# Turning batch 1's keys and queries by the DMA crossbar in two parts, loading the later batches later, and broadcasting g by a transfer

## The chip, the cores and the metric

The kernel runs on one core of a Trainium2 chip. The metric is the device time of one execution in microseconds (us), as the median of several runs. The kernel before takes 218.26 us (216.22 to 218.64, 3 runs).

A run's *state* is called slow when it lies more than 1.5% above the fastest run of the same kernel. Medians and ranges below are over all runs; ratios use fast runs alone. All other times are from one profiled execution of each kernel, counted from the start of its span.

Some words that come back: a *hole* is a stretch in which TensorE idles; a transfer *lands* when its data has arrived; to *turn* is to transpose; the *granted clock* is the recorded share of TensorE's full clock, and *half clock* a stretch in which that share is 0.50.

## The reference

Four batches of eight heads, 768 tokens, head dimension 64. Each chunk of 32 queries attends to 8 memory keys, its own chunk, 16 tokens to the left and 8 to the right. The result passes through a normalised MLP with a residual:

```python
for c in range(768 // 32):
    l_start, r_end = max(0, 32*c - 16), min(768, 32*c + 32 + 8)
    k_full = concat([mem_k, k[:, :, l_start:r_end]]); v_full = concat([mem_v, v[:, :, l_start:r_end]])
    scores = q[:, :, 32*c : 32*c+32] @ k_full.T / sqrt(64)
    out[:, :, 32*c : 32*c+32] = softmax(scores) @ v_full
x  = heads side by side            # (4, 768, 512)
xn = (x - mean) / sqrt(var + 1e-6) * g
return x + relu(xn @ w_ch1) @ w_ch2   # 512 -> 2048 -> 512
```

## The kernel before

The 24 tiles of 128 tokens are worked in eight units of three. Unit `u` runs the MLP of its own tiles; the attention of the next unit's tiles is threaded between its matmuls. The position is a *step*: steps 0 to 15 are the first matmul (`up`), 16 to 27 the second (`down`). `at(step, fn, ...)` puts a piece of other work behind that step in program order:

```python
def attend(steps, kind="dma"):
    for i, (s0, s1, s2, s3) in enumerate(steps):
        t = following[i]
        at(s0, scores, ...); at(s1, values, ...); at(s2, norm, ...)
        at(s3, turn_x, u + 1, i, t % 6, kind)     # xn -> xT, for the next unit's up
        at(min(s3 + 3, 27), root, ...)
```

The program's order is also the order in which GpSimd and SyncE issue their transfers: in the changed kernel the transposes at 102.76 us stand behind the store at 102.25 us on SyncE. A batch's keys and queries reach the layout that the scores need (`KT`, `QT`: head dimension on the partitions) in one of two ways. Batches 0 and 1 are turned by TensorE. Batches 2 and 3 come token by token and are turned by the crossbar of the DMA:

```python
def load_tokens(b, which, t):       # GpSimd's queue: 128 tokens x 8 heads
    nc.gpsimd.dma_start(out=free(dst, 512 * t, ...), in_=dram(src, ...))
def cross_k(b, half, t0, t1):       # SyncE's queue
    nc.sync.dma_start_transpose(out=free(KT[b % 2], ...), in_=kraw[b % 2][...])
def k_around(b, t0, t1): ...        # GpSimd: four copies of the neighbours' edges inside KT
def load_v_head(b, h):              # GpSimd's queue: one head's own rows of V
    nc.gpsimd.dma_start(out=V[b % 2][16:80, :, h, 0:64], in_=dram(v, ...))
def v_around(b):                    # SyncE's queue: the neighbours' rows, SBUF to SBUF
    nc.sync.dma_start(out=vt[0:16, 1:NG, :, :], in_=vt[64:80, 0 : NG - 1, :, :])
    nc.sync.dma_start(out=vt[80:88, 0 : NG - 1, :, :], in_=vt[16:24, 1:NG, :, :])
```

So batch 2 needs a chain: token loads, crossbar transposes, edge copies, value loads (behind these copies on GpSimd), neighbour copies, values. The old plan spread it over three units:

```python
elif u == 1: ...
    for t in range(6):
        for which in range(2): at(14, load_tokens, 2, which, t)
if u == 2:
    cross((0, 0, 1, 1), 2, 0, 4, 3)
    at(8, k_around, 2, 0, 4)
    for h in range(H): at(8, load_v_head, 2, h)
    cross((14, 14, 15, 15), 2, 4, 6, 6)
elif u == 3:
    at(1, v_mem, 2); at(1, v_around, 2)
    at(4, k_around, 2, 4, 6)
    # attend: scores of the first tile at step 9, its values at step 14
```

At the start TensorE runs ten filler matmuls (`stay_busy(10)`) until the memory keys and K have landed.

The softmax here doesn't subtract the row's maximum and nothing guards it: scores larger than these inputs give would overflow.

## Time and profile before

| | before |
|---|---|
| median of 3 runs | 218.26 us |
| span of the profiled run | 214.4 us |
| first up matmul of unit 0 | 19.91 us |
| lengths of units 0 to 7 | 27.22, 26.98, 23.41, 23.13, 23.27, 23.13, 23.13, 24.26 us |

A unit runs from its first `up` matmul to the next unit's. First the clock in 40 slices, then the engines' totals in units 3 and 4 (stretch, its length, busy time and instructions of PE, its weight loads, DVE, ACT and POOL, then the granted TensorE clock, the DMA share, which is summed packet time over 16 engines' time and can exceed 1, and GB/s):

```profile
PEclk9999999999999999999999999999999999999999
...
97.52:120.65 23.13, 23.13 (x209) 13.40 (x208) 11.87 (x26) 9.73 (x20) 5.19 (x10) 1.00 0.41 75
120.65:143.92 23.27, 23.27 (x210) 13.37 (x209) 11.67 (x27) 9.17 (x20) 16.91 (x27) 1.00 2.00 164
```

TensorE is busy for the whole of both (23.13 of 23.13). Batch 2's chain: SyncE's transposes, GpSimd's edge copies and value loads, and TensorE's values (start, duration, what, how often, and in brackets the idle time just before and what ended it):

```profile
75.77 2.74 SPq L253 DMA_TRANSPOSE KT<-kraw  x2
```

```profile
80.75 0.79 POOL L274 COPY KT<-KT 128x192 f16<-128x192 f16 x3 [1.03 <-DMA KT<-kraw]
81.48 5.98 POOL L122 DMA_DIRECT2D V<-in_v_dram  x8
```

```profile
108.06 0.70 PE L307 MATMUL att<-V,AT 104*64 104x65 f16 x32
...
120.65 2.11 PE L375 MATMUL mm<-xT,w1c 128*128 128x384 f16 x12
```

The value loads start at 81.48 and the values at 108.06. Neither the values nor the first up matmuls of unit 4 (the last line) wait for anything.

### The profile page before, as it was taken

Reading aid. Unit: us, or ns where it says so; the run is one execution under the profiler, and the core shown is the slowest. Engines: PE = TensorE matmul, PEld = TensorE weight load, DVE = VectorE, ACT = ScalarE, POOL = GpSimd, SP = SyncE. Lnnn points to the kernel's source line nnn. Section 1 sums busy time; section 2 is a strip of 40 time slices with the busy share of each in tenths; the row PEclk is TensorE's granted clock in tenths of the full one; section 3 lists DMA queues with packets and bytes.
Section 4 is the critical chain, followed back from the end, with each engine's and each line's share of the span. In section 5 each row is a group of like instructions: output and inputs, shape, how many; then the busy total and the mean of one; then the engine's idle time right before and its main releaser. Section 6 shows DMA issues by size and latency. Waiting matters only on the chain.

```text
span 214.4 us, 5336 instructions
## 1 busy us (share of the span) xinstructions
PE 208.1 (97%) x2173; PEld 123.6 (58%) x2173; DVE 113.2 (53%) x268; ACT 91.1 (42%) x187; POOL 91.5 (43%) x169
## 2 busy tenths in 40 slices
PE   7889999999999999999999999999999999999993
PEld 2446775457755566546654566447644665457553
DVE  3748583685747548524375349324474447534222
ACT  4255445855573677202653167103661265303200
POOL 7992244689999319810004999520121000400000
PEclk9999999999999999999999999999999999999999
DMA  5999999999999959995313999997694101330012
GB/s 79 162 128 202 206 214 185 191 206 238 145 141 172 138 163 125 115 205 139 54 26 78 144 182 153 155 170 92 168 146 132 54 3 24 85 115 0 0 52 98
DMA packets 87611, 27.26 MB, mean 127 GB/s; under 512 B 78289, under 2 KB 84081, under 8 KB 87538
## 3 DMA queue, kind: packets, MB, share of 16 engines
q0 software_dynamic: 62128, 14.38, 75.3%
q1 hardware_dynamic: 25458, 12.54, 26.4%
q8 instruction: 17, 0.28, 0.5%
q14 instruction: 8, 0.07, 0.1%
HBM read 28.84 MB, written 6.29 MB: 164 GB/s over the span
## 4 chain that ended last, share of the span: by engine, by line
PE 91%; DMA 3%; DVE 2%; POOL 1%; issue 1%; ACT 1%; POOLq 0%; DVEq 0%; ACTq 0%
PE mm L375 38%; PE mm L392 38%; PE att L307 4%; PE att L287 3%; DMA kraw<-in_k_dram 3%; PE att L187 2%; PE mm L410 2%; PE mm L364 2%; PE mm L187 1%; DVE xn L327 1%; DVE xs L318 1%; PE att L350 1%; ACT AT L294 1%; PE mm L533 0%; PE att L364 0%
## 5 line engine op out<-in xcount | busy, mean ns | idle before, releaser
L375 PE MATMUL mm<-xT,w1c 128*128 128x384 f16 (+2 forms) x528 | 87.9, 322 | 0.1
L392 PE MATMUL mm<-w2c,rT 128*128 128x512 f16 x368 | 84.2, 379 | 0.0
L375 PEld LDWEIGHTS <-w1c 128*128 128x128 f16 x528 | 57.9, 114 | 24.7 <-issue 0.6
L381 ACT ACTIVATE rT<-mm 128x384 f16<-128x384 f32 (+2 forms) x66 | 31.7, 484 | 75.2 <-PE mm L375 53.8
L392 PEld LDWEIGHTS <-rT 128*128 128x128 f16 x368 | 34.5, 98 | 38.4
L383 DVE TENSOR_SCALAR rT<-mm 128x384 f16<-128x384 f32 (+2 forms) x66 | 35.6, 542 | 33.6 <-PE mm L375 33.3
L399 DVE SCALAR_TENSOR_TENSOR osb<-mm,rstd,xs 128x512 f32<-128x512 f32 x23 | 17.3, 751 | 42.4 <-PE mm L392 31.1
L294 ACT ACTIVATE AT<-att,band 104x512 f16<-104x512 f32 x48 | 29.5, 688 | 10.9 <-PE att L287 9.2
L336 POOL TENSOR_SCALAR veps<-squares 128x1 f32<-128x1 f32 x24 | 5.2, 216 | 52.1 <-ACT junk L333 50.8
L116 POOL DMA_DIRECT2D V<-in_v_dram x24 | 19.0, 796 | 12.1 <-DMA w1c<-in_moe_w_ch_dram 8.2
L333 ACT ACTIVATE junk<-xs,nmean 128x512 f16<-128x512 f32 x24 | 17.4, 724 | 7.7 <-DVE nmean L324 6.9
L327 DVE SCALAR_TENSOR_TENSOR xn<-xs,nmean,g_row 128x512 f16<-128x512 f32 x24 | 18.0, 752 | 0.9
L318 DVE SCALAR_TENSOR_TENSOR xs<-att,rec 128x512 f32<-128x512 f32 x24 | 16.6, 691 | 0.8
L274 POOL COPY KT<-KT 128x128 f16<-128x128 f16 (+4 forms) x16 | 4.3, 294 | 23.8 <-DMA KT<-kraw 23.8
L340 POOL TENSOR_TENSOR rstd<-veps,mhalf 128x1 f32<-128x1 f32 x24 | 13.2, 551 | 2.0
L122 POOL DMA_DIRECT2D V<-in_v_dram x16 | 12.0, 804 | 0.5 <-issue 0.4
L307 PEld LDWEIGHTS <-AT 104*64 104x64 f16 x384 | 7.5, 111 | 7.2 <-issue 3.0
L247 POOL DMA_DIRECT2D qraw<-in_q_dram x12 | 11.3, 943 | 0.0
L247 POOL DMA_DIRECT2D kraw<-in_k_dram x12 | 11.3, 940 | 0.0
L307 PE MATMUL att<-V,AT 104*64 104x65 f16 x384 | 9.5, 197 | 0.6 <-ACT AT L294 0.6
L364 PE MATMUL mm<-busy 128*128 128x512 f16 x26 | 8.8, 472 | 1.2 <-DVE counts L456 1.2
L287 PEld LDWEIGHTS <-KT 64*128 64x128 f16 x384 | 6.5, 95 | 5.9 <-issue 5.8
(76 smaller groups left out, 115.0 us busy)
## 6 DMA issues: line engine op xcount, KB each, us to landing
out_dram<-osb SPq DMA_DIRECT2D x23, 256.0 KB, 2.8
V<-in_v_dram POOLq DMA_DIRECT2D x36, 96.0 KB, 6.1
w1c<-in_moe_w_ch_dram POOLq DMA_DIRECT2D x4, 512.0 KB, 10.0
w2c<-in_moe_w_ch_dram POOLq DMA_DIRECT2D x4, 512.0 KB, 15.0
kraw<-in_k_dram POOLq DMA_DIRECT2D x12, 128.0 KB, 5.4
qraw<-in_q_dram POOLq DMA_DIRECT2D x12, 128.0 KB, 5.5
qraw<-in_q_dram POOLq DMA_DIRECT2D x3, 384.0 KB, 13.5
kraw<-in_k_dram POOLq DMA_DIRECT2D x3, 256.0 KB, 5.7
```

The costliest lines, as they stand in the source:

```text
L116: nc.gpsimd.dma_start(out=V[b % 2][r : r + hi - lo, g, :, 0:64], in_=dram(v, b * H * HS + lo * D, [[64, hi - lo], [HS, H], [1, 64]]),)
L247: nc.gpsimd.dma_start(out=free(dst, 512 * t, [[64, H], [1, 64]]), in_=dram(src, b * H * HS + 128 * t * D, [[D, 128], [HS, H], [1, 64]]),)
L294: nc.scalar.activation(out=free(a, 32 * c, [[512, 2], [64, 8], [1, 32]], KR), in_=free(p, 32 * c, [[512, 2], [64, 8], [1, 32]], KR), func= ...
L307: nc.tensor.matmul(out=p[64 * gg : 64 * gg + 64, h // 4, c0 : c0 + 65], lhsT=AT[t % 3][0:KR, h % 2, 4 * gg + h // 2, :], rhs=V[b % 2][0:KR ...
L318: nc.vector.scalar_tensor_tensor(out=x.rearrange("p (h d) -> p h d", h=H), in0=free(p, 0, [[128, H], [1, 64]]), scalar=1.0, in1=free(r, 0, ...
L327: nc.vector.scalar_tensor_tensor(out=xn[i], in0=x, scalar=nmean[i], in1=g_row, op0=ALU.add, op1=ALU.mult,)
L333: nc.scalar.activation(out=junk, in_=xs[xi], func=ACTF.Square, bias=nmean[i], accum_out=squares[i],)
L375: nc.tensor.matmul(out=p, lhsT=free(w, i, [[4, 128]]), rhs=xT[u % 2][:, dt, lo:hi], start=(dt == 0), stop=(dt == 3),)
L381: nc.scalar.activation(out=o, in_=p, func=ACTF.Relu)
L383: nc.vector.tensor_scalar(out=o, in0=p, scalar1=0.0, scalar2=None, op0=ALU.max)
L392: nc.tensor.matmul(out=p, lhsT=rT[hc][:, 128 * i : 128 * i + 128], rhs=w2c[hc // 4][:, hc % 4, :], start=(hc == 0), stop=(hc == 15),)
L399: nc.vector.scalar_tensor_tensor(out=o, in0=p, scalar=rstd[t % 9], in1=xs[t % 9], op0=ALU.mult, op1=ALU.add,)
```

## The change

Its intent: take batch 1's 128 TensorE transposes off the busiest engine by using the crossbar for batch 1 as well (in two parts, tiles 0 to 3 and 4 to 5). Batch 1's tokens then need the queues at the time at which batch 2's were loaded, so batch 2's chain moves later, and the attention steps of units 1 to 3 move with it. Unit 0's and 1's square sums and roots are placed by hand. At the start, g reaches all partitions by a transfer instead of an fp32 matmul. The core of the diff:

```diff
-    nc.vector.memset(ones32, 1.0)
+    nc.sync.dma_start(out=g_row, in_=dram(moe_g_ln, 0, [[0, 128], [1, 512]]))
     nc.sync.dma_start(out=memk32, ...)
-    nc.sync.dma_start(out=g_one, in_=dram(moe_g_ln, 0, [[0, 1], [1, 512]]))
...
-    nc.tensor.matmul(out=banks[2], lhsT=ones32, rhs=g_one, start=True, stop=True)
-    vec(out=g_row, in_=banks[2])
...     # u == 0
-            for h in (0, 4):
-                for which in range(2):
-                    at(15, load_kq, 1, which, 0, 96, h, h + 4)
+            for t in range(6):
+                for which in range(2):
+                    at(15, load_tokens, 1, which, t)
...     # u == 1
-            for j in (0, 2):
-                at(5 + 3 * j, kq_block, 1, j, 0, NG, "att")
-            for t in range(6):
-                for which in range(2):
-                    at(14, load_tokens, 2, which, t)
-            attend(((16, 19, 19, 22), (16, 19, 20, 23), (21, 23, 23, 26)), "att")
+            cross((1, 1, 2, 2), 1, 0, 4, 3)
+            at(3, k_around, 1, 0, 4)
+            for g in range(6):
+                at(3, load_v_group, 1, g)
+            cross((24, 24, 25, 25), 1, 4, 6, 6)
+            attend(((18, 22, 22, 24), (18, 22, 23, 25), (23, 25, 25, 27)), "att")
...     # u == 2
+            attend(((4, 9, 9, 9), (4, 9, 10, 10), (11, 15, 15, 15)))       # was 2, 7, 7, 7 ...
-                cross((0, 0, 1, 1), 2, 0, 4, 3)
-                at(8, k_around, 2, 0, 4)
-                    at(8, load_v_head, 2, h)
-                cross((14, 14, 15, 15), 2, 4, 6, 6)
+                for g in range(6, NG):
+                    at(0, load_v_group, 1, g)
+                        at(0, load_tokens, 2, which, t)
+                cross((23, 23, 24, 24), 2, 0, 4, 3)
...     # u == 3
+            attend(((11, 18, 18, 18), (11, 18, 19, 19), (20, 24, 24, 24)))  # was 9, 14, 14, 14 ...
-                at(1, v_around, 2)
+                at(0, k_around, 2, 0, 4)
+                    at(0, load_v_head, 2, h)
+                at(11, v_around, 2)
+                cross((14, 15, 16, 17), 2, 4, 6, 6)
```

More of the change, by code (lines that the diff above doesn't have):

```diff
@@ L49 @@
     g_row = sb.tile([128, 512], FP32, name="g_row")
-    g_one = sb.tile([1, 512], FP32, name="g_one")
-    ones32 = sb.tile([1, 128], FP32, name="ones32")
     busy = sb.tile([128, 512], FP16, name="busy")
@@ L242, in place @@
     def place(b, g):
-        return g if b < 2 else g % 2 * (NG // 2) + g // 2
+        return g if b < 1 else g % 2 * (NG // 2) + g // 2
     def load_tokens(b, which, t):
@@ L331, in root, with squared @@
     def root(t, xi):
+        squared(t, xi)
+        rooted(t, xi, nc.gpsimd)
+    def squared(t, xi):
         i = t % 3
@@ L335, in root, with rooted @@
         )
-        nc.gpsimd.tensor_scalar(
+    def rooted(t, xi, eng):
+        i = t % 3
+        eng.tensor_scalar(
             out=veps[i], in0=squares[i], scalar1=1.0 / 512, scalar2=1e-6,
@@ L339, in root @@
         )
-        nc.gpsimd.tensor_tensor(out=rstd[xi], in0=veps[i], in1=mhalf, op=ALU.pow)
+        eng.tensor_tensor(out=rstd[xi], in0=veps[i], in1=mhalf, op=ALU.pow)
     def turn_x(u, i, t, kind="att"):
@@ L524 @@
         turn_kq(first_k[j], k16[0], j, CUT[0])
-    stay_busy(4, spare)
+    stay_busy(3, spare)
     for j in range(2, 4):
@@ L532 @@
         keep_q(on[j], first_q[j], 0, j, CUT[1], 0, 6)
-    nc.tensor.matmul(out=banks[2], lhsT=ones32, rhs=g_one, start=True, stop=True)
-    vec(out=g_row, in_=banks[2])
+    stay_busy(3, spare)
     scores(0, 0)
@@ L580, in attend @@
                 at(s3, turn_x, u + 1, i, t % 6, kind)
-                at(min(s3 + 3, 27), root, t % 6, t % 9)
+                if u:
+                    at(min(s3 + 3, 27), root, t % 6, t % 9)
         def cross(steps, b, t0, t1, t2):
@@ L593 @@
             at(14, nc.vector.memset, memv16[:, :, :, 64:HD], 1.0)
-            at(23, clear_v, 1, nc.gpsimd)
+            at(12, clear_v, 1, nc.gpsimd)
             for j in (0, 2):
@@ L598 @@
             for t in range(3):
-                at(19 + t, root, t, t)
-            for h in (0, 4):
-                for which in range(2):
-                    at(15, load_kq, 1, which, 0, 96, h, h + 4)
-            for g in range(6):
-                at(23, load_v_group, 1, g)
-            attend(((17, 19, 19, 22), (17, 21, 21, 24), (20, 23, 23, 26)), "att")
-            at(26, mem_cols, 1)
-            at(26, v_mem, 1)
-        elif u == 1:
-            for j in (0, 2):
-                at(5 + 3 * j, kq_block, 1, j, 0, NG, "att")
-                at(7 + 3 * j, keep_rest)
-            for g in range(6, NG):
-                at(0, load_v_group, 1, g)
+                at(12 + t, squared, t, t)
+                at(14, rooted, t, t, nc.gpsimd)
             for t in range(6):
                 for which in range(2):
-                    at(14, load_tokens, 2, which, t)
-            attend(((16, 19, 19, 22), (16, 19, 20, 23), (21, 23, 23, 26)), "att")
-        elif following:
-            if u in (2, 4):
+                    at(15, load_tokens, 1, which, t)
+            attend(((17, 19, 19, 22), (17, 21, 21, 24), (20, 23, 23, 26)), "att")
+            at(16, mem_cols, 1)
+            at(20, v_mem, 1)
+        elif u == 1:
+            for t in range(3, 6):
+                at(t - 3, squared, t, t)
+                at(2, rooted, t, t, nc.gpsimd)
+            cross((1, 1, 2, 2), 1, 0, 4, 3)
[4 more added lines that the diff above has]
+            attend(((18, 22, 22, 24), (18, 22, 23, 25), (23, 25, 25, 27)), "att")
+        elif following:
+            if u == 2:
+                attend(((4, 9, 9, 9), (4, 9, 10, 10), (11, 15, 15, 15)))
+            elif u == 3:
+                attend(((11, 18, 18, 18), (11, 18, 19, 19), (20, 24, 24, 24)))
+            elif u == 4:
                 attend(((2, 7, 7, 7), (2, 7, 8, 8), (9, 13, 13, 13)))
@@ L623 @@
             if u == 2:
-                cross((0, 0, 1, 1), 2, 0, 4, 3)
-                at(8, mem_cols, 2)
-                at(8, k_around, 2, 0, 4)
-                for h in range(H):
-                    at(8, load_v_head, 2, h)
-                cross((14, 14, 15, 15), 2, 4, 6, 6)
-            elif u == 3:
-                at(1, v_mem, 2)
-                at(1, v_around, 2)
-                at(4, k_around, 2, 4, 6)
+                at(0, k_around, 1, 4, 6)
+                for g in range(6, NG):
[4 more added lines that the diff above has]
+                cross((23, 23, 24, 24), 2, 0, 4, 3)
+                at(20, mem_cols, 2)
+            elif u == 3:
+                at(0, k_around, 2, 0, 4)
+                for h in range(H):
+                    at(0, load_v_head, 2, h)
+                at(11, v_mem, 2)
+                at(11, v_around, 2)
+                cross((14, 15, 16, 17), 2, 4, 6, 6)
+                at(23, k_around, 2, 4, 6)
                 for t in range(6):
```

## The prediction

> **What bounds the kernel now.** I read the page's busy line first, then the chain that ended last, then what TensorE waited for, then the engines' timelines in the stretch that the change touches. The kernel works in eight units of three 128-token tiles. A unit has 28 steps, steps 0 to 15 the first matmul ("up") and 16 to 27 the second ("down"), and the attention of the next unit is threaded between them. The busy line and the chain's shares by engine:
>
> ```profile
> PE 208.1 (97%) x2173; PEld 123.6 (58%) x2173; DVE 113.2 (53%) x268; ACT 91.1 (42%) x187; POOL 91.5 (43%) x169
> ...
> PE 91%; DMA 3%; DVE 2%; POOL 1%; issue 1%; ACT 1%; POOLq 0%; DVEq 0%; ACTq 0%
> ```
>
> TensorE is busy 97% and is 91% of the chain. From the pieces of the chain (start, duration, what):
>
> ```profile
> 11.67 1.05 PE mm L533 x2
> ...
> 51.19 1.48 PE att L187 x64
> ...
> 56.69 1.48 PE att L187 x64
> ...
> 87.32 10.36 PE mm L392 x48
> ```
>
> The third and second lines are batch 1's 128 TensorE transposes, 2.96 us on the chain. L533 is the fp32 matmul that broadcasts g. The last line gives a down step: 4 of 48 matmuls, 10.36/12 = 0.863 us. An up step is 3.90/6 = 0.65 us (six of them before 51.19). What the matmuls themselves waited for, in all:
>
> ```profile
> PE mm L364 <- DVE counts L456: 1.2, 1, 1.2
> PE mm L187 <- DMA kraw<-in_k_dram: 1.1, 2, 0.6
> PE att L307 <- ACT AT L294: 0.6, 1, 0.6
> ```
>
> All three lie before 15 us. From there the old schedule hides every wait, so whatever the new one exposes is a loss in full. How narrowly it hides them is seen in unit 1, VectorE first, then TensorE (start, duration):
>
> ```profile
> 66.03 0.69 DVE L318 SCALAR_TENSOR_TENSOR xs<-att,rec 128x512 f32<-128x512 f32 x1
> ...
> 67.85 0.69 DVE L318 SCALAR_TENSOR_TENSOR xs<-att,rec 128x512 f32<-128x512 f32 x1
> ...
> 69.98 0.75 DVE L399 SCALAR_TENSOR_TENSOR osb<-mm,rstd,xs 128x512 f32<-128x512 f32 x1 [0.46 <-PE mm L392]
> ```
>
> ```profile
> 68.64 0.39 PE L350 MATMUL att<-identity,xn 128*128 128x128 f16 x4
> ```
>
> There are two attention buffers in PSUM. The transpose at 68.64 takes the one that VectorE finished reading at 67.85+0.69 = 68.54: 0.1 us of slack.
>
> **What the Trainium skill says.** "TensorE: Matmul & The Clock Gate", Back-to-back issue gap, gives an isolated gap of about 216 ns for 512 columns; 863/4 = 216 ns here agrees (its sustained 131 ns isn't seen). "DMA: Bandwidth & Descriptors", DMA Transpose (X-bar), says that the plain DMA transpose can be issued only from the sync and scalar engines; here all 31 stand on SyncE's in-order queue, behind the stores. The same page, Anatomy of one DMA, puts a fixed 2 us or so on a transfer, mostly for its completion; here a value load in a quiet queue lands 2.9 us after its issue began, and a crossbar transpose about 3.5 us. The same page, Issuing engines are not separate DMA queues, says all queues share 16 engines; here token loads that land 0.84 us apart land about 1 us further apart for each output store beside them.
>
> **The change part by part.**
> *Start.* The g matmul (1.05 us) goes, and net two filler matmuls of about 0.21 us come; at most 0.55 us is gained, since the scores then wait for the Q copy that ends at 12.27. The second matmul of unit 0 starts its third part at 40.85, and its weights landed at 40.61, so about 0.2 us survives. The g transfer runs while the DMA engines are less than half busy. Sum -0.2.
>
> *Unit 1, gain.* The transposes go: -2.96.
>
> *Unit 1, tokens.* GpSimd reaches its first batch 1 load at about 37.2 + 2.4 (clearing V) + 2.8 (three roots) = 42.4 us. Twelve token loads at 0.87 each; the seventh, which the K transpose needs, is issued at 47.6. Queued behind w2 and memory values (until 44.4), with three stores beside it, it lands at about 46.5 + 6x0.84 + 3x0.94 = 54.3. SyncE then issues four transposes at 1.27-1.3 each; the last Q one starts at 58.5 and lands at 62. Scores are due at 47.1 + 16x0.65 + 0.2 + 3x0.863 = 60.3. So a wait of 0.3 to 2.2: I take +1.3. The V loads, behind the K edge copies on GpSimd, start near 61 and just make step 22.
>
> *Unit 1, norms.* Values now come at step 22 and the turning at 24, where it was 19 and 22. VectorE has two norms (1.9 us each) in that time, and now the output combine of step 23 (0.75) stands between them in program order. The second buffer comes free 0.1 + 1.9 + 0.75 + 0.93 = 3.7 us after the values, and TensorE wants it after two down steps, scores and slack, 2.25: +1.4. The third tile's values are at step 25 and its turning at 27: the norm needs 2.07 (70.48 to 72.55 before) against 1.73, +0.35; and the xT copy (ends 1.0 us after the turning starts, 73.02 to 74.02) has no step behind it any more, +0.75. Together +2.5.
>
> *Unit 2.* V groups 6 to 11 are issued at its start, behind the third root and the edge copies (GpSimd free about 76.5). The fourth is issued 2.3 later and lands 2.9 after that, 81.7; its values are due near 81.2: +0.5.
>
> *Unit 3, the largest.* Batch 2's K transposes move from step 0 to step 23 of unit 2, behind a store: they start 3.45 - 1.3 = 2.15 us before unit 3 starts. Before, the value loads began 5.7 us after K's transposes (75.77 to 81.48, the edge copies between), so they begin at +3.55; eight at 0.75, the last at +8.8, landed at +11.7. Only then can the neighbouring values be copied. SyncE before:
>
> ```profile
> 99.98 0.60 SPq L130 DMA_DIRECT2D V<-V  x1
> 100.63 1.68 SPq L131 DMA_DIRECT2D V<-V  x1
> ```
>
> The DMA between 104 and 107 us, in 40 slices of 0.075 us:
>
> ```profile
> DMA  0000000000000499809000000000000000000000
> ```
>
> Its last packets end at about 105.5, 5.5 us after the first issue. I take 4.6 for the new order, in which the memory rows no longer stand ahead: ready at +16.5. The values are due at step 18, 16x0.65 + 0.57 + 3x0.863 = +13.6: a wait of +3.0. In the old schedule they came 2 us after the packets. The third tile's values then come at step 24, and its turning by DMA landed 4.43 us after the values before (114.67 to 119.10); three steps are left, 2.6: +1.85.
>
> Sum: -0.2 - 2.96 + 1.3 + 2.5 + 0.5 + 3.0 + 1.85 = +6.0. From unit 4 on nothing is added: batch 3's loads shift about as far as TensorE does.
>
> **The rivals.** *Clean gain:* every new wait is hidden and only the removed work counts: 218.3 - 3.2 = 215.1. For it: TensorE is the bound everywhere, and the steps look chosen to fit arrivals (7 steps between the neighbour copies and the values). Against it: those steps count from step 11 of unit 3, while the loads before it can't have landed by then. *Gain given back:* unit 1's waits eat the transposes, and the batch 2 waits are small because the neighbour copies take some 3 us when nothing stands ahead of them and the loads land early: 218 to 219.5. For it: the gap of 1.5 us in the queue before the last copy's packets is unexplained. *A pile-up:* 256-byte token loads, V loads and stores in 42 to 62 us delay the scores by 3 us more, and all else follows: 225 to 227. For it: the DMA digits are at 9 until 75 us. Against: batch 1's old loads occupied the queue for about the same 10 us.
>
> **Range and chances.** Most terms are estimates from neighbouring rows, and waits in series partly cover each other (a late unit 1 gives unit 2's loads time), so I take 5 of the 6 us: 218.3 + 5 is 223.3, and since the single profiled run of before was at the low side, 216.1, I say 223.0. Low 218.5 (second rival), high 226.5 (third). 2% is 4.4 us, just under my centre: slower 0.60, within 0.37, faster 0.03.
>
> **What would show it.** The transposes of batch 1 gone from the chain, 2.96 us. TensorE's busy share down to about 95%. In unit 1, idle time before the scores, ended by the Q transpose or edge copies, and before the first turning, ended by VectorE. In unit 3, a hole of about 3 us before the values, ended by the neighbour copy, and one of nearly 2 at the start of unit 4, ended by the xT transpose. If TensorE has no hole near its 110th microsecond, the largest term is wrong, and the kernel is about even; if it has none in unit 1 either, it is 3 us faster.

## The result, and the profile after

The changed kernel takes 239.01 us (237.23 to 239.80, 3 runs): 9.6% longer, ratio 1.0956 (95% interval 1.0843 to 1.1069). A ratio here is the mean time of one kernel's fast runs over that of the other's fast runs of the same rounds, so not quite the ratio of the medians. The span of the profiled run went from 214.4 to 238.1 us, 23.7 us more.

The page of the changed kernel, the lines that answer to those of before (busy time by engine; TensorE's busy share and its granted clock in 40 slices of 6 us; the chain by engine):

```profile
PE 215.6 (91%) x2045; PEld 124.7 (52%) x2045; DVE 107.6 (45%) x254; ACT 88.3 (37%) x183; POOL 101.1 (42%) x185
...
PE   6899999999879899999808939999999999999994
...
PEclk9659999999997999999985986999999999999999
...
PE 55%; DMA 26%; POOL 12%; issue 3%; DVE 1%; SPq 1%; ACT 1%; POOLq 0%; ACTq 0%; DVEq 0%
```

TensorE has 128 instructions fewer (2173 to 2045), yet is busy 7.5 us *longer* (208.1 to 215.6). The third line says why: in slices 2, 3, 13, 21, 22, 24 and 25 the clock is below 9 tenths. Before, all 40 digits were 9. In the trace the low stretches are 7.4 to 17.6, 72.2 to 75.7, 123.4 to 130.3 and 140.5 to 147.3 us, at *half clock* (a *granted clock*, the recorded share of TensorE's full clock, of 0.50). What the matmuls waited for (us in total, times, longest; the fillers' wait at the very start and four under 1 us left out):

```profile
PE att L305 <- DMA V<-V: 7.6, 1, 7.6
PE mm L380 <- DMA xT<-xn: 4.1, 1, 4.1
PE att L305 <- DMA V<-in_v_dram: 2.3, 3, 1.2
...
PE mm L185 <- DMA kraw<-in_k_dram: 1.2, 1, 1.2
...
PE att L285 <- DMA QT<-qraw: 0.7, 2, 0.4
...
```

The two long holes, and units 3 and 4 as a whole (columns as for these units of the kernel before):

```profile
115.66 2.75 PE L397 MATMUL mm<-w2c,rT 128*128 128x512 f16 x12
125.98 1.09 PE L305 MATMUL att<-V,AT 104*64 104x65 f16 x32 [7.57 <-DMA V<-V]
127.00 3.50 PE L397 MATMUL mm<-w2c,rT 128*128 128x512 f16 x8
...
141.54 4.00 PE L380 MATMUL mm<-xT,w1c 128*128 128x384 f16 x12 [4.07 <-DMA xT<-xn]
```

```profile
104.56:141.54 36.98, 25.34 (x210) 14.05 (x208) 12.70 (x27) 9.72 (x20) 15.46 (x27) 0.89 1.15 126
141.54:167.39 25.85, 25.85 (x208) 14.20 (x209) 11.01 (x26) 9.27 (x20) 14.64 (x26) 0.89 1.61 141
```

Read the durations, not only the brackets: eight `down` matmuls take 3.50 us behind the first hole, where eight take 1.90 us at full clock. Unit 4 has no idle time (25.85 busy of 25.85), and is 2.58 us longer than before with the same number of matmuls.

The chain into the first hole, SyncE's queue and GpSimd's:

```profile
102.76 3.25 SPq L251 DMA_TRANSPOSE KT<-kraw  x2
...
120.02 0.60 SPq L128 DMA_DIRECT2D V<-V  x1
```

```profile
107.22 0.40 POOL L272 COPY KT<-KT 128x256 f16<-128x256 f16 x1 [6.33 <-DMA KT<-kraw]
108.23 0.79 POOL L272 COPY KT<-KT 128x192 f16<-128x192 f16 x3 [0.62 <-DMA KT<-kraw]
108.97 5.97 POOL L120 DMA_DIRECT2D V<-in_v_dram  x8
```

The value loads begin at 108.97, directly behind the edge copies, which waited 6.33 us for the transposes. The last load lands at 119.81, the neighbour copy goes out at 120.02 and lands at 125.79, the values start at 125.98. Each link follows the one before at once. From the value loads to the values there are now 17.0 us; before there were 26.6, with slack.

Where the 23.7 us lie, by the starts of the units:

| | before | after | difference |
|---|---|---|---|
| first up | 19.91 | 23.65 | +3.74 |
| unit 0 | 27.22 | 27.21 | 0.0 |
| unit 1 | 26.98 | 29.86 | +2.88 |
| unit 2 | 23.41 | 23.85 | +0.44 |
| unit 3 | 23.13 | 36.98 | +13.85 |
| unit 4 | 23.27 | 25.86 | +2.59 |
| units 5 to 7 | 70.52 | 70.70 | +0.2 |

### The profile page after: what moved, and what is told of

Its sections match the earlier page's. It is cut to its first block, busy times and chain, and to the rows that moved or that the text cites. A ratio compares the mean times of both kernels' runs of the same rounds, so it can differ in the third digit from the quotient of the medians.

```text
span 238.1 us, 5078 instructions
## 1 busy us (share of the span) xinstructions
PE 215.6 (91%) x2045; PEld 124.7 (52%) x2045; DVE 107.6 (45%) x254; ACT 88.3 (37%) x183; POOL 101.1 (42%) x185
## 4 chain that ended last, share of the span: by engine, by line
PE 55%; DMA 26%; POOL 12%; issue 3%; DVE 1%; SPq 1%; ACT 1%; POOLq 0%; ACTq 0%; DVEq 0%
PE mm L397 25%; PE mm L380 23%; DMA V<-in_v_dram 13%; POOL V L114 4%; DMA KT<-kraw 3%; DMA w1c<-in_moe_w_ch_dram 3%; DMA kraw<-in_k_dram 3%; PE att L305 3%; DMA V<-V 2%; DMA xT<-xn 2%; PE att L285 2%; PE mm L415 1%; POOL kraw L245 1%; POOL qraw L245 1%; POOL V L120 1%
## 5 line engine op out<-in xcount | busy, mean ns | idle before, releaser
L380 PE MATMUL mm<-xT,w1c 128*128 128x384 f16 (+2 forms) x528 | 89.4, 327 | 4.8 <-DMA xT<-xn 4.1
L397 PE MATMUL mm<-w2c,rT 128*128 128x512 f16 x368 | 87.2, 389 | 0.0
L380 PEld LDWEIGHTS <-w1c 128*128 128x128 f16 x528 | 58.5, 115 | 31.2 <-issue 7.8
L305 PE MATMUL att<-V,AT 104*64 104x65 f16 x384 | 10.5, 201 | 10.1 <-DMA V<-V 7.6
L272 POOL COPY KT<-KT 128x128 f16<-128x128 f16 (+4 forms) x24 | 6.3, 294 | 28.8 <-DMA KT<-kraw 28.8
L305 PEld LDWEIGHTS <-AT 104*64 104x64 f16 x384 | 8.2, 114 | 17.3 <-issue 14.2
L245 POOL DMA_DIRECT2D kraw<-in_k_dram x18 | 16.9, 936 | 0.3 <-DMA kraw<-in_k_dram 0.3
L245 POOL DMA_DIRECT2D qraw<-in_q_dram x18 | 16.8, 936 | 0.0
L315 DVE RECIPROCAL rec<-att 128x8 f32<-128x8 f32 x24 | 4.9, 203 | 25.9 <-PE att L305 22.2
L345 POOL TENSOR_TENSOR rstd<-veps,mhalf 128x1 f32<-128x1 f32 x24 | 13.8, 575 | 2.0
L285 PEld LDWEIGHTS <-KT 64*128 64x128 f16 x384 | 7.6, 101 | 7.8 <-issue 7.0
```

The source lines that it names most:

```text
L245: nc.gpsimd.dma_start(out=free(dst, 512 * t, [[64, H], [1, 64]]), in_=dram(src, b * H * HS + 128 * t * D, [[D, 128], [HS, H], [1, 64]]),)
L305: nc.tensor.matmul(out=p[64 * gg : 64 * gg + 64, h // 4, c0 : c0 + 65], lhsT=AT[t % 3][0:KR, h % 2, 4 * gg + h // 2, :], rhs=V[b % 2][0:KR ...
L380: nc.tensor.matmul(out=p, lhsT=free(w, i, [[4, 128]]), rhs=xT[u % 2][:, dt, lo:hi], start=(dt == 0), stop=(dt == 3),)
L397: nc.tensor.matmul(out=p, lhsT=rT[hc][:, 128 * i : 128 * i + 128], rhs=w2c[hc // 4][:, hc % 4, :], start=(hc == 0), stop=(hc == 15),)
```

## The experiments

There were fifteen runs in five groups. Each group has its own runs of the kernel before on the same chip (medians 217.57, 217.72, 217.82, 216.87 and 217.06 us). All results were correct. The theory at the outset: the lateness of batch 2's chain makes the two holes, the holes make the clock drop, and something about g makes the late start. The rivals: batch 1's own transfers do the harm, or the late start is chance.

### Batch 2's lateness alone, in the kernel before

```diff
# u == 1
-            for t in range(6):
-                for which in range(2):
-                    at(14, load_tokens, 2, which, t)
# u == 2, u == 3: as in the change (tokens at step 0, transposes at 23 and 24,
#   edges and values in unit 3, and the changed attention steps); batch 1 and g untouched
```

> The kernel before, batch 1 still turned by TensorE and g still by matmul, with only the lateness of batch 2 taken from the change: its token loads at the start of unit 2, its K and Q transposes at steps 23 and 24, its edge copies and value loads at the start of unit 3, and the attention steps that go with them. Theory A (the loss sits in batch 2's lateness): units 3 and 4 take 37 and 25.9 us as in the changed kernel, all else as before: 218 + 16 = 234. Rival B (batch 1's new token loads and crossbar transposes are what crowds the transfers and starts the loss): no more than 222.

Measured: 233.96 us (233.82 to 235.54), ratio 1.0757 (1.0683 to 1.0831). Its waits:

```profile
PE att L307 <- DMA V<-V: 7.2, 1, 7.2
PE mm L375 <- DMA xT<-xn: 4.6, 1, 4.6
```

Unit 3 takes 37.67 us and unit 4 24.58, with half clock from 116.0 to 126.2 and from 136.5 to 139.9. So the lateness without any change to batch 1 or g makes both holes and 16.2 us, most of the loss. (The profiled run is 17.9 us longer than that of the kernel before: 15.9 in units 3 and 4 and 2.2 at the start, where this run too has half clock, from 13.6 to 20.4 us. More on that below.) That batch 1's transfers cause the holes has fallen.

### Fillers in the two holes

The changed kernel with matmuls of zeros ahead of the values (34 of them) and at the end of unit 3 (20). They wait for nothing and write to a PSUM buffer of the MLP.

```diff
+        if u == 3:
+            plan[18].insert(0, (stay_busy, (34,)))
+            plan[27] = plan.get(27, []) + [(stay_busy, (20,))]
```

> The changed kernel with filler matmuls in its two longest holes: 34 (about 7.3 us) before the values of step 18 of unit 3, and 20 (4.3 us) at the end of unit 3. The waits themselves stay. Theory A (after an idle stretch TensorE's clock is halved for one to three stretches of 3.4 us, and that alone is 2.2 + 2.6 us here): the clock stays full through units 3 and 4 and the time falls by 4 to 5 us, to 234.5. Rival B (the slow matmuls after the holes are slow for another reason, such as traffic to SBUF): no gain, 238.5 to 240.

Measured: 233.42 us (232.20 to 235.80), ratio 1.0703 (1.0634 to 1.0773). The profiled run was slow because of a long wait in unit 1, so only its units 3 and 4 are read here:

```profile
118.43 7.50 PE L369 MATMUL mm<-busy 128*128 128x512 f16 x34
125.98 0.70 PE L305 MATMUL att<-V,AT 104*64 104x65 f16 x32
126.61 1.90 PE L397 MATMUL mm<-w2c,rT 128*128 128x512 f16 x8
```

The values start at the same 125.98 us as in the changed kernel, but take 0.70 us instead of 1.09, and the eight matmuls behind them 1.90 instead of 3.50. Units 3 and 4 together take 58.64 us, where the changed kernel takes 62.83, and their clock is 1.00 throughout. Nothing useful was added and the data did not come sooner, yet 4.2 us are gone: that much was half clock *behind* the holes. The medians differ by 5.6 us. The fast runs' granted clock is 0.985 to 1.000 against 0.943 to 0.957 in the changed kernel, so in some of them the start was quick as well, which these fillers don't touch.

### A short and a long hole in the kernel before

To see how long a hole must be, batch 3's neighbour copies were queued later on SyncE in unit 4, with all else as before.

```diff
                 at(17, v_mem, 3)
-                at(17, v_around, 3)
...
                 cross((20, 21, 24, 25), 3, 4, 6, 6)
+                at(20, v_around, 3)      # short: behind one K transpose.  Long: at(24, ...)
```

> The kernel before with one fault made on purpose: batch 3's neighbour copies of values queued behind the first of the late K transposes in unit 4. By the old trace they then land about 3.4 us after the values matmuls of unit 5 are due. Theory A (a hole costs its length and then half clock for at least one stretch of 3.4 us, 1.7 us more): the hole of 2 to 4 us costs 4 to 6 us in unit 5. Rival B (a hole as short as that leaves the clock alone): the hole's length and nothing more, 2 to 4 us.

> As the former, with the neighbour copies behind the Q transposes as well: by the old trace a hole of about 7.5 us in unit 5. Theory A: hole of 6 to 9 us, then half clock for two stretches of 3.4 us from the hole's middle on, 2 to 3.5 us more than the hole, 228 to 230 in all. Rival B: the hole's length alone, 225 to 227, with the matmuls after it at their usual 216 ns each.

Measured, short: 218.33 us (217.18 to 221.89), ratio 0.9998 (0.9935 to 1.0062). Long: 224.65 us (222.99 to 227.08), ratio 1.0343 (1.0269 to 1.0417). First the short hole, then the long one:

```profile
156.42 0.70 PE L307 MATMUL att<-V,AT 104*64 104x65 f16 x32 [1.24 <-DMA V<-V]
...
157.73 1.03 PE L392 MATMUL mm<-w2c,rT 128*128 128x512 f16 x4
```

```profile
159.70 0.85 PE L307 MATMUL att<-V,AT 104*64 104x65 f16 x32 [4.74 <-DMA V<-V]
...
161.74 1.89 PE L392 MATMUL mm<-w2c,rT 128*128 128x512 f16 x4
```

After 1.24 us of idle time four matmuls take 1.03 us, as always; the unit is 1.3 us longer, which is the hole. After 4.74 us the same four take 1.89, and the unit is 6.4 us longer (29.54 against 23.13): 4.74 for the hole, 1.7 for one stretch of half clock, 160.1 to 163.5. The short hole came out below the range that I had expected, so it serves as the case in which nothing happens.

The traces of all runs, taken together, say a little more. After the first up there are 17 holes of 3.25 to 7.79 us, and in each of them half clock begins, inside the hole or at most 0.4 us after it. Below that it is mixed: one of 2.47 us (in the next run) was followed by none, nor were two close together of 0.66 and 1.53 us (the best-ordered kernel); 0.69 and 1.18 us (the changed kernel, unit 1) or 0.87 and 1.38 us (K's tokens first) were. So the length of a short hole does not decide it alone, and what does is not shown.

### Batch 2's value loads one unit earlier

```diff
# u == 2
                         at(0, load_tokens, 2, which, t)
+                for h in range(H):
+                    at(0, load_v_head, 2, h)
# u == 3
-                for h in range(H):
-                    at(0, load_v_head, 2, h)
```

> The changed kernel with batch 2's value loads issued in unit 2 behind its token loads, instead of at the start of unit 3 behind the K edge copies; nothing else. Theory A (the values are late only because their loads are issued behind the K transposes and edge copies): the 7.6 us wait on the neighbour copies in unit 3 goes, and with it the half clock after it (2.2 us): about 229; the wait for the third tile's turning at the start of unit 4 stays at 2 to 4 us. Rival B (the transfer queue is full, the loads land late wherever they are issued): 235 to 239.

Measured: 231.28 us (230.68 to 235.42), ratio 1.0615 (1.0566 to 1.0663).

```profile
PE mm L380 <- DMA xT<-xn: 4.4, 1, 4.4
PE att L285 <- POOL KT L272: 2.5, 1, 2.5
```

The wait for the neighbour copies falls from 7.6 to 0.5 us, and unit 3 from 36.98 to 31.29. But the scores now wait 2.5 us for the edge copies, and the wait at the start of unit 4 is still there (4.4 us). A link was taken out of the chain and the next one showed.

### All of batch 2's values ahead of its tokens

The same idea taken to its end: value loads ahead of the tokens, neighbour copies in unit 2, and the old attention steps in unit 3.

```diff
-                attend(((11, 18, 18, 18), (11, 18, 19, 19), (20, 24, 24, 24)))
+                attend(((9, 14, 14, 14), (9, 14, 15, 15), (16, 20, 20, 20)))
# u == 2
-                for g in range(6, NG):
-                    at(0, load_v_group, 1, g)          # now in unit 1, step 3
+                for h in range(H):
+                    at(0, load_v_head, 2, h)           # ahead of the tokens
+                at(16, v_mem, 2); at(16, v_around, 2)
```

> The changed kernel with the value loads moved ahead of what they don't depend on: batch 1's groups 6 to 11 behind groups 0 to 5 in unit 1, batch 2's heads ahead of its tokens in unit 2, the neighbour copies at step 16 of unit 2, and unit 3's attention back at the old steps (9, 14, 16, 20). Theory A (what units 3 and 4 lose is late values, the late third tile and the clock after them): no wait over 1 us in unit 3, full clock there, units 3 and 4 about 23.3 us each; 239 - 16.3 = 222.7, still slower than before by what unit 1 and the start lose. Rival B (any order of these loads is too much for the queue at that time): over 230.

Measured: 235.04 us (233.92 to 239.16; the profiled run slow), ratio 1.0768 (1.0690 to 1.0845). A miss by 12 us. A second edit to it, the second tile's norm ahead of the output combine in unit 1:

```diff
-            attend(((18, 22, 22, 24), (18, 22, 23, 25), (23, 25, 25, 27)), "att")
+            attend(((18, 22, 22, 24), (18, 22, 22, 25), (23, 25, 25, 27)), "att")
```

> The former kernel with the second tile's norm of unit 1 at step 22, so that it stands ahead of the output combine of step 23 on VectorE; nothing else. Theory A (TensorE's wait of about 1.06 us before the first turning of unit 1, which three runs show ended by VectorE, comes from that order): the wait falls to under 0.3 us and the time by 0.7 to 1 us. Rival B (the wait is for late values, wherever the norm stands): no change within 0.3 us.

Measured: 235.22 us (234.82 to 235.56), ratio 1.0793 (1.0739 to 1.0847). Its profiled run was fast, so the miss is read there, SyncE's queue first, then the waits:

```profile
100.38 7.52 SPq L251 DMA_TRANSPOSE KT<-kraw  x2
108.07 2.58 SPq L257 DMA_TRANSPOSE QT<-qraw  x2
```

```profile
PE att L285 <- DMA QT<-qraw: 6.5, 2, 5.4
PE mm L380 <- DMA xT<-xn: 5.2, 1, 5.2
```

The values are there in time, but K's transposes still stand at step 23 of unit 2 behind the stores and take 7.52 us to issue (3.25 in the changed kernel), and Q's stand behind them: issued at 108.07, landed at 112.73, with the scores due at 107.3. The hole of 7.6 us at the values had become one of 5.4 at the scores, and the clock dropped as before. The small edit did what the prediction said of it (the wait before unit 1's first turning fell from 1.05 to 0.40 us, the unit from 26.27 to 25.61), and the total did not move. Where the 0.65 us went is not shown: the only profile without the small edit is of a slow run.

### K's tokens first in batch 1's queue

The kernel of the last run, with this and with batch 1's values issued ahead of the K edge copies:

```diff
+    clear_v(1, nc.gpsimd)                # early, between the w2 loads
-            for t in range(6):
-                for which in range(2):
-                    at(15, load_tokens, 1, which, t)
+            for which, t in [(0, 0), (0, 1), (0, 2), (0, 3), (1, 0), (1, 1), (1, 2)]:
+                at(15, load_tokens, 1, which, t)
+            for which, t in [(0, 4), (0, 5), (1, 3), (1, 4), (1, 5)]:
+                at(15, load_tokens, 1, which, t)
```

> The former kernel with batch 1's arrival sped up: V's clearing moved to where GpSimd waits for weights, the four K token tiles loaded ahead of the Q ones, the values of batch 1 issued ahead of the edge copies. Theory A (unit 1 waits for Q's transpose and for values only because the tokens start late and K's transpose needs the seventh load): no wait before scores or values in unit 1, unit 1 at most 25 us against 27.0 of before, total 218 to 220 with a good start. Rival B (the crossbar transposes are slow because the queue is full, whatever the order): Q or values are still waited for, unit 1 26 us or more.

Measured: 237.07 us (234.35 to 241.19, two of four slow), ratio 1.0790 (1.0698 to 1.0881), no gain. The scores of unit 1 still wait 0.65 us for Q, and unit 2 waits 0.87 and 1.38 us more. That fits the rival, a queue that is full whatever its order; this run tries one order.

### The crossbar for batch 1, batch 2 at its old times

The most favourable order that I could find: batch 1 by the crossbar, K's transposes already in unit 0, batch 2's chain and steps as before.

```diff
+            for half in range(2):
+                at(24, cross_k, 1, half, 0, 4)      # u == 0
...
+                    at(4, load_tokens, 2, which, t)  # u == 1
...   # units 2 and 3: the plan of the kernel before
```

> The changed kernel's crossbar turning of batch 1, with batch 2 back at the old kernel's times: K tokens 0 to 3 first, then Q 0 to 2 and the first values, K's transposes ahead of unit 0's stores on SyncE, the second pair of transposes early in unit 1, batch 2's tokens in unit 1, and the old kernel's attention steps in units 1 to 3. Theory A (the crossbar turning itself is a gain of the transposes' 2.96 us, and all the loss is the order and lateness of what goes with it): no TensorE wait over 0.3 us after unit 0, unit 1 about 24.0 us, units 2 to 4 as before, 218 - 2.9 = 215. Rival B (turning batch 1 by transfers crowds the queue in any order): Q, edges or values are waited for in unit 1 or 2, 219 or more.

Measured: 221.59 us (221.20 to 222.36, 6 runs), ratio 1.0172 (1.0128 to 1.0217). No holes of over 1.6 us and no half clock after the first up, so 17 us are back. But it is 3.8 us slower than the kernel before, where 3 us of gain were hoped for. Its profile waits 2.2 us for Q's transposes in unit 1, 0.9 for edge copies and 1.2 for neighbour copies; and its first up lies at 23.42 us, 3.5 later than before. That pointed back to the start.

### The g transfer behind the memory keys and values

```diff
-    nc.sync.dma_start(out=g_row, in_=dram(moe_g_ln, 0, [[0, 128], [1, 512]]))
     nc.sync.dma_start(out=memk32, ...)
     nc.sync.dma_start(out=memv32, ...)
+    nc.sync.dma_start(out=g_row, in_=dram(moe_g_ln, 0, [[0, 128], [1, 512]]))
```

> The changed kernel with the transfer of g behind the two memory loads on SyncE's queue instead of ahead of them; nothing else. Theory A (the g transfer delays the memory keys, TensorE idles 2.1 of 2.3 us around 5 to 7.2 us, and its clock is halved for 10 us): the first up step moves back from 23.65 to about 20 us, all clock up to there is full, and the time falls by about 3.7 us to 235.3. Rival B (the clock drop at the start is a matter of where the clock's window happens to lie, or comes from the missing g matmul): still low clock between 7 and 17 us and 238 to 240 us.

Measured: 237.82 us (235.33 to 239.19), ratio 1.0868 (1.0774 to 1.0961), first up at 24.70: no better start. The memory keys no longer waited, but K landed at 8.3 us instead of 7.2, and TensorE waited 2.4 us for it. In this profile the record of the clock begins only at 17.4 us, and the missing stretch counts as full; K's 32 transposes took 1.06 us, where they take 0.69 at full clock, so it was at half clock there as well. Moving the transfer behind the other two did not help.

### The g transfer alone, in the kernel before

```diff
-    nc.sync.dma_start(out=g_one, in_=dram(moe_g_ln, 0, [[0, 1], [1, 512]]))
+    nc.sync.dma_start(out=g_row, in_=dram(moe_g_ln, 0, [[0, 128], [1, 512]]))   # first on SyncE
-    nc.tensor.matmul(out=banks[2], lhsT=ones32, rhs=g_one, start=True, stop=True)
-    vec(out=g_row, in_=banks[2])
```

> The kernel before with only the g part of the change: g by transfer, queued first on SyncE, no g matmul, the fillers moved as in the change. Theory A (g ahead of the memory keys costs the start): about 3.5 us slower than before, 221.8, with half clock from 7 to 17 us. Rival B: 0 to 0.5 us faster than before, 217.8 to 218.3.

Measured: 219.77 us (216.77 to 220.61), ratio 1.0012 (0.9924 to 1.0099). Two of the four runs (220.61 and 220.4 us) were sorted out as slow, and two fast runs can't exclude 1%. What was sorted out was the effect itself. The profiled run is the one of 220.61 us; its clock is listed as 1.000, but its record begins at 17.5 us, and until then the matmuls take the durations of half clock:

```profile
6.42 1.06 PE L185 MATMUL mm<-identity,kraw 64*64 64x64 f16 x32 [0.48 <-DMA kraw<-in_k_dram]
```

Its first up came at 22.96 us. Repeated with five rounds:

> The kernel before with only g by transfer, repeated with more rounds. Theory A: 217.8 + 2.5 = 220.3, ratio 1.011 or above. Theory B: ratio 1.000 within 0.005.

Measured: 220.11 us (218.80 to 221.43, all six fast), ratio 1.0159 (1.0115 to 1.0203), so about 3.3 us lost by this edit alone. All six have a granted clock of 0.974 to 0.984; the fast runs of the kernel before have 0.992 to 1.000 in the same rounds (one that was sorted out as slow, at 220.01 us, has 0.984). The start of this run and of the kernel before, then the stretch from 8.7 to 18.9 us in this run and in the kernel before (columns as for the units above):

```profile
5.96 0.25 PE L165 MATMUL mm<-identity,memk 128*64 128x64 f16 x4 [0.41 <-ACT memk L466]
7.56 0.69 PE L185 MATMUL mm<-identity,kraw 64*64 64x64 f16 x32 [1.35 <-DMA kraw<-in_k_dram]
...
6.38 0.69 PE L187 MATMUL mm<-identity,kraw 64*64 64x64 f16 x32 [0.64 <-DMA kraw<-in_k_dram]
```

```profile
8.70:18.90 10.20, 10.15 (x157) 5.29 (x157) 3.70 (x8) 4.30 (x9) 7.94 (x12) 0.50 1.91 166
```

```profile
8.70:18.90 10.20, 9.13 (x186) 4.75 (x185) 6.50 (x16) 5.79 (x12) 7.97 (x11) 1.00 1.48 150
```

Half a microsecond before K's first load there is now the issue of a transfer that writes 128 rows of 2 KB; K landed at 7.52 instead of 6.34 us. TensorE sits idle for 0.41 and 1.35 us, and then runs 10.2 us at half clock although it is busy for 10.15 of them. The first up moves from 19.91 to 23.68 us. Is it the later landing that costs, or the idle time? Five more fillers in these two gaps decide it:

```diff
-    stay_busy(10)
+    stay_busy(11)
...
+    stay_busy(4, spare)
     for j in range(2):
         turn_kq(first_k[j], k16[0], j, CUT[0])
```

> The kernel before with g by transfer, and five filler matmuls more in the gaps before the memory keys' and K's first transposes (one and four). Theory A (the idle gaps hold TensorE at half clock): the clock comes up near 7 us, the first up lies at 20 to 21.3, granted clock about 0.99, and the ratio to the kernel before falls from 1.016 to 1.004 to 1.008 (the later landing of K, 1.2 us, stays). Theory B (the later landing and crowding alone): ratio 1.014 to 1.018, first up above 23.

Measured: 216.31 us (215.86 to 216.96), ratio 0.9965 (0.9925 to 1.0006): all of it comes back, and more than I had expected. First up at 19.66 us, a granted clock of 0.997 to 1.000 in all six runs.

```profile
8.70:18.90 10.20, 9.55 (x209) 5.20 (x204) 6.75 (x17) 6.22 (x12) 8.76 (x12) 1.00 1.53 157
```

So the idle time before the first transposes, and the half clock behind it, were what this edit cost. It is level with the kernel before; the interval just includes 1. (In this profile K landed early, at 6.08 us, so how late K came in the other five runs isn't known.)

But the g transfer is not the only thing that can bring half clock at the start. The run with batch 2's lateness alone has the old broadcast, word for word, and TensorE's only gap from 5.3 to 13.8 us is one of 0.65 us, which the profile of the kernel before has as well. Yet its three fillers behind that gap (first line) take 1.46 us, and those of the kernel before (second line) 0.82:

```profile
14.43 1.46 PE L364 MATMUL mm<-busy 128*128 128x512 f16 x3
...
14.86 0.82 PE L364 MATMUL mm<-busy 128*128 128x512 f16 x3
```

Over all profiles: with the transfer issued first and no added fillers at the start, the first up lies at 22.96 to 23.70 us in eight and at 20.31 in one; with the matmul it lies at 19.18, 19.76, 19.91, 20.63, 22.07 and 22.98. So the transfer makes a late start likely, and chance makes some without it. The same five fillers in the kernel before, without the transfer, were not run, nor were they run in the best-ordered kernel.

### g by the matmul again, in the two crossbar kernels

The reverse test: the old broadcast of g put back into the changed kernel, and into the best-ordered one.

```diff
-    nc.sync.dma_start(out=g_row, in_=dram(moe_g_ln, 0, [[0, 128], [1, 512]]))
+    nc.sync.dma_start(out=g_one, in_=dram(moe_g_ln, 0, [[0, 1], [1, 512]]))     # behind memk32
+    nc.tensor.matmul(out=banks[2], lhsT=ones32, rhs=g_one, start=True, stop=True)
+    vec(out=g_row, in_=banks[2])
```

> The changed kernel with g broadcast by a matmul as in the kernel before, nothing else. Theory A: 239.0 - 2.8 = 236.2, first up at 19 to 22. Theory B: 239.0 within 1 us.

> The best-ordered kernel (batch 1 by the crossbar, batch 2 as before) with g broadcast by a matmul as in the kernel before. Theory A: the g transfer makes the start late; profiled starts say about 2.8 us (mean first up 23.2 with the transfer, 20.4 with the matmul). Then the first up is at 19 to 22 and the time 221.6 - 2.8 = 218.8, within 1% of the kernel before. Theory B: the start is chance; then 221.6 again, 1.7% above the kernel before.

Measured: 239.74 us (238.74 to 241.23), ratio 1.1076 (1.1032 to 1.1120), and 223.68 us (223.37 to 225.57), ratio 1.0334 (1.0291 to 1.0378). Both theories missed: neither kernel got faster, and the second got slower, though its first up came at 19.76 us as theory A said. Its profile shows why: unit 1 grew from 26.20 to 33.54 us. TensorE before and behind its scores, then the DMA engines' busy share from 47 to 67 us in 40 slices:

```profile
57.87 1.03 PE L399 MATMUL mm<-w2c,rT 128*128 128x512 f16 x4
64.45 0.40 PE L287 MATMUL att<-QT,KT 64*128 64x64 f16 x8 [5.56 <-DMA QT<-qraw]
```

```profile
DMA  9999999999993999999999999999999999999999
```

TensorE reached the scores 3 us sooner than in the best-ordered kernel, but Q's transposes did not: the scores start at 64.45 here and at 62.83 there. The DMA engines read 9 tenths in nearly every slice here and in the best-ordered kernel alike. SyncE issued Q's transposes at 55.39 us, against 53.21 there, and GpSimd the first of batch 1's token loads at 40.22 against 38.42: they came later although TensorE was earlier, and why is not shown. The earlier start became a hole of 5.56 us, and the hole 10.2 us of half clock (61.0 to 71.2). In the changed kernel the profiled start at 22.98 shows a second way to lose it: there K's *second* part came late, TensorE waited 1.29 us at 10 us, and the clock was half from 12.7 to 19.5.

## Why the prediction was wrong

The direction was right, and the two holes stood where they had been put, behind the causes named. The size was wrong by a factor: +6.0 us as summed (5 taken), against +23.7 in the span. The step that failed first is a term that was not in the sum: **the prediction costed every wait as the idle time only and every matmul at its full-speed duration.** The prediction had no clock in it at all. Of the 17.7 us missed, 4.8 are half clock in units 3 and 4, some 2 lie in unit 1 and nearly 4 at the start (with up to 1.7 and some 3.3 of half clock); the remaining 6.8 are the two waits of unit 3, rightly named but put at 4.85 and measured at 11.6.

Term by term, from the profiles:

| term | predicted | profile |
|---|---|---|
| start | -0.2 | +3.7 |
| batch 1's transposes gone | -2.96 | they are gone |
| unit 1, waits for Q | +1.3 | +0.7 |
| unit 1, values' loads | 0 | +1.9 |
| unit 1, norms | +2.5 | +0.9 (2.0 where nothing else waits) |
| unit 1, the rest, mostly half clock | - | +2.3 |
| unit 2, value loads | +0.5 | +0.4 |
| unit 3, neighbour copies | +3.0 | +7.6 |
| third tile's turning | +1.85 | +4.1 |
| unit 3, half clock | - | +2.2 |
| unit 4, half clock | - | +2.6 |

- **The start.** "the g transfer runs while the DMA engines are less than half busy" was read from the old kernel, whose first slice of 5.4 us shows 5 tenths; in the changed kernel the transfer's packets ran from 1.8 to 4.9 us, and K landed behind them at 7.2 us, not 6.3. (Over the profiles, K landed at 6.1 to 7.5 us in the ten with the transfer first and at 5.5 to 6.4 in the six with the matmul.) Idle gaps opened, and the half clock that followed cost 3.3 us in the timed repetition. The fillers in the gaps bring that back in full. Why the *changed* kernel did not gain from getting its matmul back is shown for the best-ordered kernel (a later wait takes it) and not for the changed one, whose second K load came late in the one profile.
- **Unit 1.** The sum was +0.8 and the unit grew by 2.88. The 2.3 us of rest is what remains of 2.88 + 2.96 - 0.7 - 1.9 - 0.9; the half clock from 72.2 to 75.7 us accounts for up to 1.7 of it. "V loads ... just make step 22" failed: they were 0.69 and 1.18 us late, and these two gaps, 1.9 us in all with one matmul between, are followed by the low stretch. That they caused it is not shown: in the best-ordered kernel two gaps of 2.2 us in all are followed by none. The norm term was right as a mechanism: with nothing else in the way, as in the run with the early value loads, the three waits named measure 1.06, 0.28 and 0.67 us.
- **Unit 2** was right: +0.5 predicted, 0.41 us of waiting, +0.44 in the unit.
- **Unit 3's hole.** The links were the right ones, but two were too short. The loads began 4.4 us into the unit instead of 3.55, and the last landed at 15.25 instead of 11.7. The prediction used "lands 2.9 after" for a value load in a quiet queue. The trace of the kernel before had the answer for exactly these eight loads (min, median, max):

```profile
DMA to landing us min/median/max: 2.9/5.9/6.3
```

  I had taken the minimum, which is the first load's alone. The changed kernel's loads took 5.6 to 6.6, median 6.3. The neighbour copy took 5.8 us instead of my 4.6; "memory rows no longer stand ahead" made it no shorter. (Two small slips stand there as well: 11.7 and 4.6 are 16.3, not 16.5, and the old values came 2.6 us after the packets, not 2.)
- **The third tile's turning** took 4.6 us from issue to landing beside batch 3's token loads, against 2.4 in the kernel before; 1.85 became 4.07.
- **Half clock in units 3 and 4.** 2.2 and 2.6 us. The fillers brought 4.2 of these 4.8 us back, so this part is shown, not argued. It is also the part that makes a miss by a few microseconds into one by 10%: the long hole in the kernel before cost 6.4 us where 4.74 were idle.
- **The rivals.** "A pile-up" said the right thing of batch 1's queue (token loads, value loads and stores delay the scores), at the wrong size, and for the best-ordered kernel "Gain given back" is near what happened: 2.2 + 0.9 + 1.2 us of waits against 2.96 gained, on top of the start.

Two reasons to move on from the crossbar for batch 1 follow. The lateness that it brings to batch 2 costs 16 us, and without that lateness the transfers of batch 1 are waited for in queues that are already full; no order tried here beat the kernel before. (Of the best-ordered kernel's loss of 3.8 us, 3.5 in its profile is the late start; with the fillers that cure it elsewhere it might come out level, an estimate that was not run.) Not settled: why the low stretch is one, two or three times 3.41 us long, and how much of the changed kernel's own late start is the g transfer. Its profile and most of its relatives' show the late start, but the run with fillers in the holes had a quick one (first up at 20.31 us) with the same code, and the run with the lateness alone a late one (22.07) with the old code, so chance has a part in it.

## What to carry to other kernels

Cost a wait of several microseconds on the critical path of a kernel bound by TensorE as the idle time *plus* the half clock behind it, and look at the clock row first when TensorE's busy time goes up while its work goes down. Check the row against the durations of known matmuls, since its record can begin late, and look at what was sorted out as slow: it can be the effect that is sought. Before moving a chain of transfers later, add up its links with the medians of the loaded queue, not with the shortest time in the trace, and compare the sum with the steps left. Where a wait can't be avoided, matmuls of zeros in the gap can be worth it: five of them turned a loss of 1.6% into none here.

## What the Trainium skill lacked or had wrong

- "TensorE: Matmul & The Clock Gate", Part 1, What's actually happening, says that half rate comes after at least one idle window of about 3.4 us. The quantum agrees: all low stretches before the last microseconds of a run are 3.41, 6.83 or 10.24 us here, and all 17 holes of 3.25 us or more brought one. But far less idle time was followed by half clock too: 0.41 + 1.35 us at the start, 0.69 + 1.18 us in unit 1, and in the run with the lateness alone one gap of 0.65 us, with TensorE busy for 2.99 of the 3.40 us before the drop. Single holes of 1.24 and 2.47 us were not. No page gives lengths for the shorter gaps that do it.
- The same section says that full rate comes after some 3.4 us of sustained work. Here TensorE was busy for 10.15 of 10.20 us at the start and stayed at half clock for all of them, which cost 1.6% of the kernel with g by transfer. About 3.2 us of that work were transposes, which Part 4 of the same page does not count as busy in the same way; no run here separates the two, so this is a case to add, not an error shown.
- "DMA: Bandwidth & Descriptors", Anatomy of one DMA, gives, for transfers that GpSimd issues, about 2 us plus the bytes at 436 GB/s. A value load of 96 KB took 6.3 us beside seven others, where that gives 2.2 (an estimate from the page). The page does not cover there what SyncE issues: an SBUF to SBUF copy of 220 KB took 5.8 us.
- No page gives the time of a crossbar transpose in a loaded queue. Batch 1's took 8.0 to 9.6 us from issue to landing beside token loads and stores in the best-ordered kernel; in a quiet queue the prediction had read about 3.5 us.
